# Contiguous value casts, means on the matmul engine, keys in natural order and GpSimd kept to the norm's Newton steps, in a Sinkhorn-attention and Fourier-mix kernel

## The chip, the cores and the metric

The kernel runs on one core of a Trainium2 chip. The metric is device time in microseconds (us), the median over separate executions. The engines are named as in the profile: PE (TensorE matmul), PEld (its weight loads), DVE (VectorE), ACT (ScalarE), POOL (GpSimd), SP (SyncE). A profile is one execution; its span is some 2 us shorter than the measured time. A run that is over 1.5 per cent above the fastest of its kernel is called slow.

## The reference, cut to what matters

```python
P = sort_net                                   # (4, 8, 8, 8): batch, head, block, block
for _ in range(5):                             # Sinkhorn: rows, then columns
    P = exp(P - max(P)); P /= P.sum(-1); P /= P.sum(-2)
k_sorted = einsum('bhij,bhjcd->bhicd', P, k_b) # keys and values of 8 blocks of 96 are mixed
v_sorted = einsum('bhij,bhjcd->bhicd', P, v_b)
attn = softmax(q_b @ k_sorted.T / 8)           # each block of 96 queries sees its own block
x = (attn @ v_sorted)                          # -> (4, 768, 512)
X = real(fft(fft(x, axis=1), axis=2))          # Fourier mix over rows and columns
u = x + X;  un = (u - mean(u)) / sqrt(var(u) + 1e-6)
out = u + relu(un @ w_ch1) @ w_ch2             # 512 -> 2048 -> 512
```

## The kernel before

Batches 0 and 1 share the first half of V, batches 2 and 3 the second. The kernel subtracts the mean over the 96 rows of each source block from V, so that `exp(s) - 1` can be multiplied with it in fp16; the aim is to keep digits. The mean goes through the Fourier transform by a separate path of a few rows (`a_path`, `a_rows`). A scheduler orders the instructions of each engine from the program's dependences; each engine then runs its list in that order.

```python
    # V: mean by strided reduce, then centring, halves split between DVE and GpSimd
    def v_center(t):
        for hf in range(2):
            nc.vector.tensor_reduce(                                   # L274
                vs2[:, hf, :], vh[hf].rearrange("p c d -> p d c"), axis=AX.X, op=ALU.add)
        # ... sum of the halves, times 1/96 ...
        vo = vc16[:, 0:D * BLK].rearrange("p (d r c) -> p c r d", r=6, c=16)
        for hf in range(2):
            eng = nc.vector if hf == 0 else nc.gpsimd
            eng.tensor_tensor(vo[:, 8 * hf:8 * hf + 8], ...,           # L286
                              op=ALU.subtract)   # fp16 written with a 192-byte step along d

    # attention, for each head pair
            # keys mixed on PE, evicted from PSUM row by row (c innermost, contiguous)
            dst = ks[:, :, 3 * half:3 * half + 3, :].rearrange("p i r c -> p r i c")
            if half == 0: nc.scalar.copy(dst, src)                     # L389
            else:         nc.vector.tensor_copy(dst, src)              # L391
            # q transposed on PE out of a copy that GpSimd made
            for h2 in range(2):            # one head after the other
                # 2 x (4 score matmuls, Exp on ACT, minus 1 on DVE (L423))
                # 12 AV matmuls, 65 columns wide; normalise

    # Fourier mix: fold on DVE (plus part) and GpSimd (minus part), then PE

    # layer norm: reciprocal square root by three Newton steps, all on DVE
            for _ in range(3):
                nc.vector.tensor_tensor(z, y, y, op=ALU.mult)
                nc.vector.scalar_tensor_tensor(z, z, -0.5, x, op0=ALU.mult, op1=ALU.mult)
                nc.vector.scalar_tensor_tensor(y, z, 1.5, y, op0=ALU.add, op1=ALU.mult)
    # then un (DVE), four PE transposes per 128 rows, ut (DVE), and the MLP on PE
```

The softmax here doesn't subtract the row's maximum and nothing guards it: scores larger than these inputs give would overflow.

## Time and profile before

| | before |
|---|---|
| time, median of 3 runs | 455.73 us (455.05 to 459.06) |
| span of the profile, mean granted clock | 452.6 us, 0.896 |
| first MLP matmul | 172.9 us |
| last matmul ends | 448.1 us |

The kernel has two phases. Up to the first MLP matmul, batch 0 has to go through sorting, attention, Fourier mix and norm with little for PE to do. From then on the MLP of one batch is interleaved with the attention of the next, and PE is nearly always busy. The table of stretches shows that (columns: stretch, its length, busy time and instructions of each engine, granted PE clock, DMA share, GB/s):

```profile
0.00:60.00 60.00, 2.87 (x14) 2.87 (x14) 47.86 (x39) 2.56 (x6) 26.93 (x22) 1.00 0.96 241
60.00:120.00 60.00, 15.99 (x147) 13.72 (x146) 56.00 (x39) 8.36 (x21) 35.49 (x11) 0.74 0.06 9
120.00:173.00 53.00, 32.28 (x279) 21.48 (x279) 36.16 (x82) 8.95 (x20) 17.37 (x14) 0.59 0.18 23
...
172.90:448.10 275.20, 258.74 (x1987) 144.24 (x1985) 161.63 (x395) 99.64 (x217) 56.27 (x49) 0.97 0.15 35
```

In the first phase DVE is the busy engine, not PE. The timeline shows with what (columns: start, duration, engine, line, operation, out<-in, shapes, and in brackets the idle time before it and who ended it). These are the DVE and POOL lines of the centring and of the exp-minus-1 that came after it:

```profile
19.19 30.08 DVE L286 TENSOR_TENSOR vc_127<-v_83,vb_215 128x3072 f16<-128x3072 f32 x1
19.14 15.45 POOL L286 TENSOR_TENSOR vc_127<-v_85,vb_215 128x3072 f16<-128x3072 f32 x1 [8.94 <-DVE vb_215 L280]
...
89.48 15.40 DVE L286 TENSOR_TENSOR vc_127<-v_962,vb_1579 128x3072 f16<-128x3072 f32 x1
89.47 30.14 POOL L286 TENSOR_TENSOR vc_127<-v_964,vb_1579 128x3072 f16<-128x3072 f32 x1 [0.19 <-POOL rb_105 L347]
104.45 15.39 DVE L423 TENSOR_SCALAR ebuf_119<-ex_403 96x384 f16<-96x384 f32 x1
```

In the first pair POOL ends at 34.6 and DVE at 49.3, 14.7 us later; in the second DVE ends at 104.9 and POOL at 119.6, again 14.7 us later. Whichever was second took twice as long: the two did not run side by side, one waited for the other. The exp-minus-1 on DVE, 0.49 us elsewhere, ends at 119.84, just after POOL does. By what means one engine holds up the other, the traces do not show.

### The profile page before, as it was taken

Reading aid. Unit: us, or ns where it says so; the run is one execution under the profiler, and the core shown is the slowest. Engines: PE = TensorE matmul, PEld = TensorE weight load, DVE = VectorE, ACT = ScalarE, POOL = GpSimd, SP = SyncE. Lnnn points to the kernel's source line nnn. Section 1 sums busy time; section 2 is a strip of 40 time slices with the busy share of each in tenths; the row PEclk is TensorE's granted clock in tenths of the full one; section 3 lists DMA queues with packets and bytes.
Section 4 is the critical chain, followed back from the end, with each engine's and each line's share of the span. In section 5 each row is a group of like instructions: output and inputs, shape, how many; then the busy total and the mean of one; then the engine's idle time right before and its main releaser. Section 6 shows DMA issues by size and latency. Waiting matters only on the chain.

```text
span 452.6 us, 6022 instructions
## 1 busy us (share of the span) xinstructions
PE 309.8 (68%) x2420; PEld 182.3 (40%) x2420; DVE 302.2 (67%) x553; ACT 119.5 (26%) x264; POOL 136.1 (30%) x96
## 2 busy tenths in 40 slices
PE   0000065400366459996999999979999979999996
PEld 0000065300244325653554655545456544545452
DVE  3999858999857677689654857858277777451101
ACT  1000005200122103631340753323146403406150
POOL 8390010499521910325500042290001082000000
PEclk9999999955555579999899999969999979999999
DMA  9999520200035000442001023500010000010101
GB/s 285 302 216 190 199 98 2 35 0 0 0 38 70 0 0 2 58 75 56 25 0 48 24 36 46 109 25 0 25 47 1 25 25 23 2 51 21 70 1 70
DMA packets 16549, 26.00 MB, mean 57 GB/s; under 512 B 1220, under 2 KB 11656, under 8 KB 16008
## 3 DMA queue, kind: packets, MB, share of 16 engines
q0 software_dynamic: 11040, 10.49, 15.4%
q1 hardware_dynamic: 5336, 13.55, 8.1%
q10 hardware_dynamic: 144, 1.57, 1.0%
q8 instruction: 19, 0.31, 0.3%
q14 instruction: 10, 0.08, 0.1%
HBM read 29.80 MB, written 6.29 MB: 80 GB/s over the span
## 4 chain that ended last, share of the span: by engine, by line
PE 42%; DVE 40%; DMA 7%; POOL 4%; issue 4%; ACT 2%; SPq 0%; DVEq 0%; ACTq 0%
DVE vc_127 L286 10%; DVE ebuf_119 L423 5%; DMA v_962<-in_v_dram 3%; POOL pmt_135 L456 3%; DMA v_85<-in_v_dram 2%; DVE ebuf_121 L423 2%; DVE vsb_131 L307 1%; DVE vs_1_1576 L274 1%; DVE vs_0_212 L274 1%; PE pm_2760 L563 1%; PE pm_4167 L563 1%; PE pm_3821 L563 1%; PE pm_2895 L563 1%; PE pm_1969 L563 1%; PE pm_4013 L563 1%
## 5 line engine op out<-in xcount | busy, mean ns | idle before, releaser
L556 PEld LDWEIGHTS <-w1sb 128*128 128x128 f16 x512 | 48.8, 98 | 31.6 <-issue 1.0
L242 PE MATMUL pf_180<-id_sb,pdup_178 32*128 32x32 f32 x16 | 3.6, 397 | 57.1 <-DVE pdup_178 L233 57.1
L286 POOL TENSOR_TENSOR vc_127<-v_964,vb_1579 128x3072 f16<-128x3072 f32 x1 | 30.1, 30142 | 0.2 <-POOL rb_105 L347 0.2
L286 DVE TENSOR_TENSOR vc_127<-v_83,vb_215 128x3072 f16<-128x3072 f32 x1 | 30.1, 30080 | 0.0
L242 PEld LDWEIGHTS pf_180<-id_sb,pdup_178 32*128 32x128 f32 x16 | 3.5, 325 | 57.1 <-DVE pdup_178 L233 57.1
L431 PEld LDWEIGHTS <-ebuf_119 96*128 96x128 f16 x192 | 8.5, 105 | 43.1 <-DVE ebuf_119 L423 42.5
L431 PE MATMUL pf_414<-vsb_129,ebuf_119 96*128 96x65 f16 x12 | 0.9, 244 | 31.3 <-DVE ebuf_119 L423 31.3
L286 POOL TENSOR_TENSOR vc_127<-v_85,vb_215 128x3072 f16<-128x3072 f32 x1 | 15.5, 15452 | 8.9 <-DVE vb_215 L280 8.9
L286 DVE TENSOR_TENSOR vc_127<-v_962,vb_1579 128x3072 f16<-128x3072 f32 x1 | 15.4, 15405 | 0.0
L423 DVE TENSOR_SCALAR ebuf_119<-ex_403 96x384 f16<-96x384 f32 x1 | 15.4, 15390 | 0.0
L218 ACT ACTIVATE pw<-pw 32x64 f32<-32x64 f32 x5 | 1.3, 255 | 51.2 <-DVE pw L225 50.1
L298 PEld LDWEIGHTS <-vc_127 128*128 128x128 f16 x128 | 9.9, 110 | 9.0 <-issue 8.1
L431 PEld LDWEIGHTS <-ebuf_121 96*128 96x128 f16 x192 | 8.7, 105 | 10.8 <-DVE ebuf_121 L423 10.3
L350 POOL COPY bdd_2965<-bdv_1_208 128x256 f32<-128x256 f32 x1 | 0.4, 397 | 41.6 <-PE pf_2038 L354 41.6
L393 POOL COPY qr_3090<-q_2954 128x768 f16<-128x768 f16 x1 | 0.8, 822 | 31.1 <-PE pf_2998 L398 31.1
L411 PEld LDWEIGHTS <-ksb_123 64*128 64x128 f16 x128 | 6.8, 100 | 7.6 <-issue 5.9
L567 DVE TENSOR_TENSOR u_3503<-pm_4129,u_3503 128x512 f32<-128x512 f32 x1 | 0.7, 691 | 13.2 <-PE pm_4129 L563 13.2
L416 ACT ACTIVATE ex_437<-pf_432 96x384 f32<-96x384 f32 x1 | 0.5, 486 | 32.0 <-PE pf_432 L411 32.0
L411 PEld LDWEIGHTS <-ksb_125 64*128 64x128 f16 x128 | 7.0, 103 | 4.7 <-issue 3.2
L274 DVE TENSOR_REDUCE vs_1_1576<-v_962 128x64 f32<-128x3072 f32 x1 | 5.3, 5289 | 5.3 <-DMA v_962<-in_v_dram 5.3
L567 DVE TENSOR_TENSOR u_3429<-pm_3975,u_3429 128x512 f32<-128x512 f32 x1 | 0.7, 692 | 11.2 <-PE pm_3975 L563 11.2
L237 POOL COPY pdup_190<-pw 32x1024 f32<-32x1024 f32 x1 | 1.5, 1547 | 21.8 <-DVE pw L225 21.8
(1455 smaller groups left out, 949.0 us busy)
## 6 DMA issues: line engine op xcount, KB each, us to landing
w1sb<-in_moe_w_ch_dram POOLq DMA_DIRECT2D x1, 2048.0 KB, 35.7
w2sb<-in_moe_w_ch_dram POOLq DMA_DIRECT2D x1, 2048.0 KB, 57.5
v_83<-in_v_dram ACTq DMA_DIRECT2D x1, 1536.0 KB, 6.8
v_85<-in_v_dram SPq DMA_DIRECT2D x1, 1536.0 KB
v_962<-in_v_dram SPq DMA_DIRECT2D x1, 1536.0 KB, 13.1
v_964<-in_v_dram SPq DMA_DIRECT2D x1, 1536.0 KB, 16.3
cd_sb<-k_cd SPq DMA_DIRECT2D x1, 514.0 KB
sd_sb<-k_sd SPq DMA_DIRECT2D x1, 514.0 KB
```

The costliest lines, as they stand in the source:

```text
L237: nc.gpsimd.tensor_copy(pdup.rearrange("p i (g j) -> p i g j", j=NB), pw[:, :, None, :].broadcast_to([32, NB, 16, NB]))
L242: nc.tensor.matmul(ps[:, i, :], pdup[:, i, :], id32)
L274: nc.vector.tensor_reduce(vs2[:, hf, :], vh[hf].rearrange("p c d -> p d c"), axis=AX.X, op=ALU.add)
L286: eng.tensor_tensor(vo[:, 8 * hf:8 * hf + 8], vh[hf].rearrange("p (c r) d -> p c r d", r=6), vb[:, 0:1, :][:, None, :, :].broadcast_to([12 ...
L298: nc.tensor.matmul(ps[:, dd, :], vc16[:, BLK * d:BLK * d + 128], bdv16[t].rearrange("p g i -> p (g i)"))
L307: nc.vector.tensor_copy(dst, src)
L411: nc.tensor.matmul(ps[:, j, :], ks[rows, 4 * g + j].rearrange("p r c -> p (r c)"), qt[rows, :, cc])
L423: nc.vector.tensor_scalar(ed, ex.rearrange("p j r c -> p j c r"), -1.0, None, op0=ALU.add)
L431: nc.tensor.matmul(po[:, 65 * T:65 * T + 65], e[:, S * g + 256 * tt + 128 * n: S * g + 256 * tt + 128 * n + 128], vs[:, 8 * h + 4 * g + tt ...
L456: nc.gpsimd.tensor_tensor(m_[:, :, 0:DM], rt[:, 0:3, :], rt[:, 3:6, :], op=ALU.subtract)
L556: nc.tensor.matmul(ps, w1sb[:, c, 128 * fc:128 * fc + 128], ut[:, c, :], start=(c == 0), stop=(c == 3))
L563: nc.tensor.matmul(ps, hr[:, fc, 128 * tt:128 * tt + 128], w2sb[:, fc, :], start=(fc == 0), stop=(fc == 15))
```

## The change

The intent is to take the long strided work off DVE and POOL in the first phase and to shorten the attention chain.

- V is cast to fp16 contiguously: for the first half on ACT without subtracting the mean, whose share PE then subtracts in `v_mix` (64 more matmuls); for the second half on DVE, with a tree of adds for the mean. The mean of the first half is 12 fp32 products with an identity on PE.
- Keys stay in natural order, so the mixed keys are evicted with a 12-byte step.
- GpSimd loses the folds, the reversed copies and the q copies. It gets the Newton steps of the norm.
- The scores of two heads are computed together, half of the exp-minus-1 moves to ACT, and AV streams are 96 columns wide instead of 65 (the result layout lets them overlap).

The diff, cut to its core:

```diff
-    def v_center(t):                                # strided reduces and centring, gone
+    def v_mean(t):
+        if t == 0:
+            for n in range(12):
+                nc.tensor.matmul(ps..., idf, v32[t, n // 6][...], start=(n == 0), stop=(n == 11))
+        else:
+            # 3 adds of 1024 and 4 adds of 1536 to 192 elements on DVE
+    def v_cast(t):
+        for n in range(8):
+            if t == 0: nc.scalar.copy(dst, src)
+            else:      nc.vector.tensor_tensor(dst, src, vbs[t]..., op=ALU.subtract)
     def v_mix(t):
-                nc.tensor.matmul(ps[:, dd, :], vc16[:, BLK * d:BLK * d + 128], bdv16[t]...)
+                nc.tensor.matmul(ps[:, dd, :], vcx[:, :, d], bd, ...)     # weights: 128-byte step
+                if t == 0:
+                    nc.tensor.matmul(ps[:, dd, :], vbn[:, d:d + 1].broadcast_to([128, 128]), bd, ...)
...
-                dst = ks[:, :, 3 * half:3 * half + 3, :].rearrange("p i r c -> p r i c")
+            dst = ks[:, :, 0:BLK].rearrange("p i (c r) -> p r i c", r=6)[:, 3 * half:3 * half + 3]
...
-            nc.gpsimd.tensor_copy(
+        nc.vector.tensor_copy(
             qr, q16[:, 2 * hl:2 * hl + 2].rearrange("p h r d -> p r h d"))
...
+                if h2 == 0: nc.vector.tensor_scalar(ed, src, -1.0, None, op0=ALU.add)
+                else:       nc.scalar.activation(ed, src, AF.Identity, bias=negone[0:96])
...
-                            po[:, 65 * T:65 * T + 65],
+                        po[:, 65 * T:65 * T + 96],
...
+            nc.gpsimd.tensor_scalar(xh, x, -0.5, None, op0=ALU.mult)
             for _ in range(3):
-                nc.vector.tensor_tensor(z, y, y, op=ALU.mult)
-                nc.vector.scalar_tensor_tensor(z, z, -0.5, x, ...)
-                nc.vector.scalar_tensor_tensor(y, z, 1.5, y, ...)
+                nc.gpsimd.tensor_tensor(z, y, y, op=ALU.mult)
+                nc.gpsimd.tensor_tensor(z, z, xh, op=ALU.mult)
+                nc.gpsimd.tensor_scalar(z, z, 1.5, None, op0=ALU.add)
+                nc.gpsimd.tensor_tensor(y, z, y, op=ALU.mult)
```

## The prediction

> **What bounds the kernel now.** Two phases. Until 172.9 us (first MLP matmul, timeline) PE is mostly idle: the stretch table gives it 2.9 us busy in 0-60, 0.1 in 105-120. From 172.9 on PE is busy 68.7 of 74.3, 76.9 of 82.8, 73.1 of 78.0 and 40.1 of 44.6 us: PE-bound.
>
> The chain of waits in phase one: the centring write with a 2-byte stride (L286) holds DVE 30.0 us (19.2-49.3) while only one of five Sinkhorn rounds is done; the scheduler then pulls the second half's reduce and centring (5.3 + 5.4 + 15.4 us) ahead of attention; GpSimd's 30.1 us share makes one DVE exp-minus-1 take 15.4 us instead of 0.49 (105-120); attention of batch 0 takes 7.75 us per head pair; FFT, norm 25 us.
>
> [...] besides that 15.4 us, DVE's mirrored add takes 2.9-3.3 us for 771 elements beside GpSimd work, though the 1536-element add took 0.97.
>
> **The change, costed (estimates from these durations).**
> - Removed: L286 (30 + 15.4 on DVE, 45.6 on POOL), strided reduces (21.3), the POOL collision.
> - Added at the start: 12 fp32 means on PE. The 257-wide fp32 product takes two records of 0.21 us, so 512 wide about 0.85 warm: 10-13 us. ACT casts, 8 x about 0.8 us, hidden. v_mix(0) gets 64 more matmuls: 8-11 us instead of 6.3.
> - The order of instructions shows a new risk: a DVE copy of q stands in front of the Sinkhorn sums. Before, q landed at 20 us; now perhaps 17-18, so Sinkhorn ends near 27 rather than the 12 it could.
> - Then transposes to 32 us, means to 44, first scores to 48, v_mix to 57, attention of batch 0 (about 6.3 us per pair, since two heads' exps share one chain) to 78, FFT and norm (DVE alone, with 7 us of second-half centring interleaved) to 108.
> - Phase two: PE work nearly equal. 12 AV matmuls take 0.70 us, 0.058 each, near the 0.055 of 128-column v_mix matmuls, so they look bound by the stationary side[...]. So 96-wide streams are free. Saved: about 1 us per batch of row products (L354), perhaps 1 us of scores, and 2-3 us per FFT, where PE now waits for GpSimd's pmt, ee and oo (3.9 + 1.8 + 1.9 us). ACT gains about 8 us per batch, POOL's norm chain is a little slower; both hidden by MLP.
>
> **Sum.** First MLP matmul from 172.9 to about 108: -65. Phase two 280 to about 268: -12. 452.6 - 77 = 376 span, about 378 us in time. Nearly all removed phase-one time is on the critical path; half comes back as Sinkhorn delay, means and v_mix.
>
> Predicted 378 us, 80% range 358 to 400. Faster by over 2%: 0.97; within: 0.02; slower: 0.01.
>
> **What would show it.** DVE idle 8-14 us near 4-18 us, released by q's DMA; PE busy with means 32-44; no DVE instruction over 3 us; first MLP matmul at 100-115; attention of batch 0 6-6.7 us per pair; AV spacing still about 0.06 us; PE idle before the FFT matmuls under 2 us in batches 1-3; the last stretch unchanged.
>
> **What would make it wrong.** Faster if q lands early or attention reaches 5 us per pair; slower if weight loads with a 128-byte column step cost more than contiguous ones, the second v load or the row DMAs arrive late (norm of batch 0 waits), ACT becomes the attention's limit, or the PE clock stays at half rate longer (it read 0.50 from 105 to 147).

The sum came to 378 us in time (452.6 - 65 - 12 = 376 of span, and 2 outside it). "96-wide streams are free" rests on the spacings of 0.058 and 0.055 us alone and is the author's estimate (experiment 5 tests it). Its "warm", like "cold" in an expectation below, stands for the granted clock: 1.00 or 0.50 in the traces.

## More of the kernel before

The norm's Newton steps on DVE take 0.16 us each and follow each other at 0.20 us:

```profile
163.76 0.17 DVE L522 TENSOR_SCALAR nx_848<-mv_814 128x3 f32<-128x3 f32 x1
...
164.37 0.16 DVE L529 TENSOR_TENSOR nz_850<-ny_849 128x3 f32<-128x3 f32 x1
164.57 0.16 DVE L530 SCALAR_TENSOR_TENSOR nz_850<-nz_850,nx_848 128x3 f32<-128x3 f32 x1
164.76 0.16 DVE L532 SCALAR_TENSOR_TENSOR ny_849<-nz_850,ny_849 128x3 f32<-128x3 f32 x1
...
166.14 0.55 DVE L537 TENSOR_SCALAR un_864<-u_821,mv_814,ny_849 128x512 f16<-128x512 f32 x1
```

and the evictions of the mixed keys take half a microsecond on either engine:

```profile
181.66 0.48 ACT L389 CAST ksb_123<-pf_985 128x384 f16<-128x384 f32 x1
...
181.52 0.56 DVE L391 CAST ksb_123<-pf_993 128x384 f16<-128x384 f32 x1 [1.05 <-PE pf_993 L380]
```

## The result, and the profile after

| | before, same rounds | after |
|---|---|---|
| time, median of 4 runs | 455.39 us (453.6 to 459.06) | 410.08 us (409.12 to 411.62) |
| span, granted clock | 452.6 us, 0.896 | 408.5 us, 0.923 |
| first MLP matmul | 172.9 us | 121.1 us |
| first MLP matmul to last matmul | 275.2 us | 283.5 us |

The ratio is 0.8999 (95 per cent interval 0.8936 to 0.9061). A ratio is the mean time of one kernel's fast runs over the mean time of the other's fast runs of the same rounds, so it is not quite the ratio of the medians. The change is a clear gain, but 410 us lies outside the predicted range of 358 to 400. The last two rows say where the miss of 32 us sits: the first phase was predicted to end at 108 us and ended at 121.1 (+13); the second was predicted to shrink by 12 and grew by 8 (+20).

The same stretches as before:

```profile
0.00:60.00 60.00, 27.65 (x210) 19.80 (x210) 23.95 (x57) 20.98 (x33) 23.47 (x31) 1.00 0.94 224
60.00:121.00 61.00, 35.61 (x296) 23.58 (x297) 43.99 (x88) 17.51 (x28) 6.45 (x16) 0.64 0.30 66
...
121.10:404.60 283.50, 252.87 (x1947) 141.71 (x1945) 143.60 (x304) 127.22 (x237) 25.82 (x99) 0.97 0.15 34
```

In the second phase PE has 5.9 us less to do than before (252.87 against 258.74) and yet needs 8.3 us more. The idle time of PE between its matmul records, put down to the kind of matmul that came after each gap, tells which wait grew:

| PE idle after the first MLP matmul, us, in front of | before | after |
|---|---|---|
| the Fourier mix | 10.3 | 0.0 |
| the transposes of the normalised rows | 3.1 | 16.3 |
| AV | 1.7 | 9.7 |
| the MLP's first product | 0.7 | 3.8 |
| all | 16.5 | 30.6 |

The Fourier mix behaves as predicted. The norm does not: the transposes of its output now wait 16.3 us. The POOL timeline shows the chain, and the PE timeline what it did to PE:

```profile
170.69 0.17 DVE L585 TENSOR_SCALAR nx_1504<-mv_1470 128x3 f32<-128x3 f32 x1
170.95 0.24 POOL L586 TENSOR_SCALAR nh_1507<-nx_1504 128x3 f32<-128x3 f32 x1 [20.30 <-DVE nx_1504 L585]
171.35 0.19 POOL L593 TENSOR_TENSOR nz_1506<-ny_1505 128x3 f32<-128x3 f32 x1 [0.15 <-DVE ny_1505 L589]
171.62 0.20 POOL L594 TENSOR_TENSOR nz_1506<-nz_1506,nh_1507 128x3 f32<-128x3 f32 x1
171.90 0.23 POOL L595 TENSOR_SCALAR nz_1506<-nz_1506 128x3 f32<-128x3 f32 x1
172.22 0.20 POOL L596 TENSOR_TENSOR ny_1505<-nz_1506,ny_1505 128x3 f32<-128x3 f32 x1
...
174.72 0.55 DVE L600 TENSOR_SCALAR un_1525<-u_1477,mv_1470,ny_1505 128x512 f16<-128x512 f32 x1 [3.46 <-POOL ny_1505 L596]
```

```profile
175.32 0.40 PE L605 MATMUL pf_1527<-idh_sb,un_1525 128*128 128x128 f16 x4 [2.38 <-DVE un_1525 L600]
175.56 0.33 PE L619 MATMUL pm_1936<-ut_1009,w1sb 128*128 128x384 f16 x1
```

From the variance term to the normalised rows, the norm took 2.4 us before (163.76 to 166.14) and takes 4.0 us here (170.69 to 174.72); where a cast on DVE runs beside it, as in the group at 125 us, it is 4.8 us. There are thirteen GpSimd instructions in place of nine on DVE, and they follow each other at 0.27 to 0.32 us instead of 0.20. PE waits 2.38 us at 175.32 although more of the MLP (L619, at 175.56) stands right behind: what it multiplies had been complete since 132.9 us. PE takes its matmuls in order, and the scheduler had put the transposes there. Over the seven groups the wait grew by 1.9 us each, close to the 1.6 us by which the chain grew.

The first phase again, from the start. The DVE copy of q, predicted as a risk, is there, and it has a second side (DVE, POOL and DVE lines):

```profile
17.57 3.28 DVE L440 COPY qr_266<-q_86 128x768 f16<-128x768 f16 x1 [14.17 <-DMA q_86<-in_q_dram]
...
13.72 6.92 POOL L208 MEMSET vsf<- 1x8192 f16 x1
...
64.12 0.34 DVE L440 COPY qr_609<-q_124 128x768 f16<-128x768 f16 x1
```

The same copy takes 0.34 us when POOL is idle. At 17.57 it runs until 20.85, 0.2 us after GpSimd's memset of one partition ends (20.64): the same blocking as before, started now by a memset. The sorting then ends at 29.3 us (27 predicted). After it comes what was predicted of PE, almost to the microsecond (PE timeline):

```profile
30.02 0.39 PE L265 MATMUL pf_193<-idh_sb,pdup_189 32*128 32x32 f16 x8 [30.02 <-DVE pdup_189 L256]
...
33.93 7.47 PE L298 MATMUL pf_225<-v_78,idf_sb 128*128 128x512 f32 x12
41.23 5.31 PE L298 MATMUL pf_225<-v_81,idf_sb 128*128 128x512 f32 x12
46.48 0.36 PE L427 MATMUL pf_250<-bdk_202,k_84 128*64 128x128 f16 x6
```

| end of, us | predicted | after |
|---|---|---|
| sorting | 27 | 29.3 |
| means on PE | 44 | 46.5 |
| first scores begin | 48 | 49.1 |
| value mixing of the first half | 57 | 59.3 |
| attention of batch 0 | 78 | 83.9 |
| Fourier mix and norm (first MLP matmul) | 108 | 121.1 |

Against the prediction, the delay grows by 3.6 us between the value mixing and the end of attention, and by 7.2 us in the Fourier mix and norm. In attention, the evictions of the mixed keys stand out. They answer to L389 and L391 of before:

```profile
132.99 1.46 ACT L436 CAST ksb_118<-pf_1043 128x384 f16<-128x384 f32 x1 [4.69 <-PE pf_1043 L427]
...
133.31 1.45 DVE L438 CAST ksb_118<-pf_1051 128x384 f16<-128x384 f32 x1 [0.36 <-PE pf_1051 L427]
```

They take three times as long as before, on both engines, for the same elements. In the Fourier mix and norm, the chain of waits runs through work of the second half of V (L308 and L313 are its mean, L600 is the end of batch 0's norm; columns: start, share of the chain in us, engine, tile and line):

```profile
101.75 1.11 DVE vcx L308
102.86 0.60 DVE st_907 L577
103.47 1.12 DVE vcx L308
104.59 0.09 DVE mv_876 L578
104.68 1.70 DVE vcx L313
...
112.22 0.55 DVE un_931 L600
```

### The profile page after: what moved, and what is told of

It reads as the page before. It is cut to its first block, busy times and chain, and to the rows that moved or that the text cites. A ratio compares the mean times of both kernels' runs of the same rounds, so it can differ in the third digit from the quotient of the medians.

```text
span 408.5 us, 6064 instructions
## 1 busy us (share of the span) xinstructions
PE 316.2 (77%) x2452; PEld 185.1 (45%) x2452; DVE 212.2 (52%) x449; ACT 165.7 (41%) x298; POOL 55.7 (14%) x146
## 3 DMA queue, kind: packets, MB, share of 16 engines
HBM read 30.92 MB, written 6.29 MB: 91 GB/s over the span
## 4 chain that ended last, share of the span: by engine, by line
PE 52%; DVE 18%; ACT 13%; DMA 6%; POOL 5%; issue 5%; POOLq 0%; DVEq 0%
DMA q_86<-in_q_dram 4%; PE pf_225 L298 3%; ACT ebuf_114 L476 3%; ACT ebuf_106 L476 2%; DVE ksb_118 L438 1%; PE pf_790 L387 1%; ACT ksb_118 L436 1%; PE pf_206 L278 1%; PE pm_3686 L626 1%; PE pm_4186 L626 1%; PE pm_3840 L626 1%; PE pm_2026 L626 1%; PE pm_2933 L626 1%; PE pm_4167 L626 1%; PE pm_4148 L626 1%
## 5 line engine op out<-in xcount | busy, mean ns | idle before, releaser
L619 PEld LDWEIGHTS <-w1sb 128*128 128x128 f16 x512 | 48.7, 99 | 34.5 <-issue 5.4
L347 PEld LDWEIGHTS <-vcx 128*128 128x128 f16 x128 | 15.6, 187 | 0.1
L622 ACT ACTIVATE hr_1775<-pm_1776 128x384 f16<-128x384 f32 x1 | 0.5, 491 | 32.2 <-DVE ny_990 L587 32.2
L440 DVE COPY qr_266<-q_86 128x768 f16<-128x768 f16 x1 | 3.3, 3283 | 14.2 <-DMA q_86<-in_q_dram 14.2
L491 PEld LDWEIGHTS <-ebuf_110 97*128 97x128 f16 x96 | 5.3, 106 | 8.9 <-DVE ebuf_110 L474 8.9
L491 PEld LDWEIGHTS <-ebuf_102 97*128 97x128 f16 x96 | 5.1, 102 | 8.5 <-DVE ebuf_102 L474 7.2
L350 PEld LDWEIGHTS <-vbn 128*128 128x128 f16 x64 | 8.7, 135 | 0.0
L622 ACT ACTIVATE hr_3743<-pm_3744 128x384 f16<-128x384 f32 x1 | 0.5, 491 | 18.8 <-PE pm_3744 L619 18.8
L233 ACT ACTIVATE pw<-pw 32x64 f32<-32x64 f32 x5 | 1.3, 255 | 15.9 <-DVE pw L240 15.3
L491 PEld LDWEIGHTS <-ebuf_114 97*128 97x128 f16 x96 | 5.5, 108 | 4.8 <-ACT ebuf_114 L476 4.6
L630 DVE TENSOR_TENSOR u_3517<-pm_4148,u_3517 128x512 f32<-128x512 f32 x1 | 0.7, 691 | 13.2 <-PE pm_4148 L626 13.2
L298 PE MATMUL pf_225<-v_78,idf_sb 128*128 128x512 f32 x12 | 7.5, 787 | 0.0
L626 PEld LDWEIGHTS <-hr_1929 128*128 128x128 f16 x48 | 4.7, 98 | 5.6
L626 PEld LDWEIGHTS <-hr_2836 128*128 128x128 f16 x48 | 4.7, 98 | 5.5
L626 PEld LDWEIGHTS <-hr_4051 128*128 128x128 f16 x48 | 4.7, 98 | 5.5
L626 PEld LDWEIGHTS <-hr_3897 128*128 128x128 f16 x48 | 4.7, 98 | 5.5
L626 PEld LDWEIGHTS <-hr_3743 128*128 128x128 f16 x48 | 4.7, 98 | 5.6
L626 PEld LDWEIGHTS <-hr_3589 128*128 128x128 f16 x48 | 4.7, 102 | 5.2 <-issue 0.3
L208 POOL MEMSET vsf<- 1x8192 f16 x1 | 6.9, 6922 | 0.1
## 6 DMA issues: line engine op xcount, KB each, us to landing
w1sb<-in_moe_w_ch_dram POOLq DMA_DIRECT2D x1, 2048.0 KB, 16.5
tab_775<-k_sd SPq DMA_DIRECT2D x1, 514.0 KB, 15.8
```

What stands on the lines that cost most here:

```text
L208: nc.gpsimd.memset(vsb[96:97, :, 0:D], 0.0)
L298: nc.tensor.matmul(ps.rearrange("p c d -> p (c d)"), idf, v32[t, n // 6][:, 8 * (n % 6):8 * (n % 6) + 8, :].rearrange("p c d -> p (c d)"), ...
L347: nc.tensor.matmul(ps[:, dd, :], vcx[:, :, d], bd, start=True, stop=(t == 1))
L350: nc.tensor.matmul(ps[:, dd, :], vbn[:, d:d + 1].broadcast_to([128, 128]), bd, start=False, stop=True)
L491: nc.tensor.matmul(po[:, 65 * T:65 * T + 96], e[:, S * g + 256 * tt + 128 * n: S * g + 256 * tt + 128 * n + 128], vsf[:, vi:vi + 96], star ...
L619: nc.tensor.matmul(ps, w1sb[:, c, 128 * fc:128 * fc + 128], ut[:, c, :], start=(c == 0), stop=(c == 3))
```

## The experiments

All kernels below start from the changed kernel ("after") and gave the reference's result, except where said. Each was timed in 4 to 6 runs beside runs of the kernel before. "Idle" is PE's idle time after the first MLP matmul, as in the table above.

### 1. The norm's Newton steps back on DVE (e1_norm_dve)

My theory was that the GpSimd norm is the second phase's loss. The rival was that ACT's new work, or the wider AV, delays PE, and the norm only shows it.

```diff
-            nc.gpsimd.tensor_scalar(xh, x, -0.5, None, op0=ALU.mult)
-                nc.gpsimd.tensor_tensor(z, y, y, op=ALU.mult)
-                ... three more on gpsimd
+                nc.vector.tensor_tensor(z, y, y, op=ALU.mult)
+                nc.vector.scalar_tensor_tensor(z, z, -0.5, x, op0=ALU.mult, op1=ALU.mult)
+                nc.vector.scalar_tensor_tensor(y, z, 1.5, y, op0=ALU.add, op1=ALU.mult)
```

> One undo: the twelve small operations of the reciprocal root return from GpSimd to DVE as nine. Theory A (the norm's latency on GpSimd is what PE waits for before its transposes; PE idle before them is 16.3 us after the first MLP matmul, 3.1 in the kernel before): that idle falls to about 4 us, time about 398, most of it in batches 1 to 3; in batch 0 nothing, because the chain then shares DVE with the second half's centring. Theory B (the attention is held by ACT, and the norm's wait only moves): the idle moves to the AV matmuls, time within 3 us of 410.

Measured: 389.44 us (388.89 to 390.44), ratio to before 0.8534 (0.851 to 0.8559). That is 20.6 us less than after. The idle time before the norm's transposes fell from 16.3 to 2.0 us, and all idle time from 30.6 to 13.2. The PE and stretch views:

```profile
124.87 4.71 PE L618 MATMUL pm<-ut,w1sb 128*128 128x384 f16 x28
129.72 0.40 PE L604 MATMUL pf<-idh_sb,un 128*128 128x128 f16 x4
...
124.90:383.90 259.00, 245.82 (x1947) 138.21 (x1945) 150.57 (x363) 127.41 (x237) 6.25 (x8) 1.00 0.16 37
```

What follows: the second phase goes from 283.5 to 259.0 us, a gain of 24.5. About 17 us are idle time, and 7 us are PE's own busy time, 252.9 to 245.8 for the same 1947 matmuls. The granted clock in that stretch rose from 0.97 to 1.00. The stretch views of after tie the fall of the clock to the waits, here for the wait that ended at 259.01 us (stretch, length, busy time of the engines, then the granted clock):

```profile
256.55:259.96 3.41, 0.95 (x11) 0.71 (x12) 1.52 (x4) 0.49 (x1) 1.32 (x7) 1.00 0.16 61
259.96:263.37 3.41, 3.41 (x14) 1.58 (x13) 1.12 (x3) 0.49 (x1) 0.00 (x0) 0.50 0.00 0
```

In after, three of the seven waits (ended at 259.01, 286.42 and 331.55) are followed within a microsecond by such a half-rate stretch of 3.41 us; in experiment 1 none is. In all sixteen traces the clock changes on a grid of 3.41 us. In the second phases, a full-rate stretch of that grid in which PE was idle for 59 per cent or more, by its matmul records, was followed by half rate 32 times out of 32; one with 58 per cent or less never was (1175 stretches, 19 of them 30 per cent idle or more). Before and after alone have 7 of the 32, at 62 per cent or more, and 143 of the others, at 50 per cent or less. So a wait of 2.1 to 2.5 us costs some 1.7 us more, or nothing, depending on how it falls on the grid (an estimate: half of 3.41 us). Three such stretches, and the 6.83 us at half rate from 126.84 less the 2.5 us of waiting in them, come to about 7 us, which is PE's extra busy time.

The theory stands: experiments 3 and 5 take back the two rival changes and leave the waits before the transposes at 15.8 and 15.9 us. One thing is not separated. Each build is scheduled anew, and PE's list changed with the edit: the transposes of the second of the seven groups stand after 68 products of the MLP's first stage in after, and after 86 here. No run kept the norm on GpSimd and put its transposes later. One thing went the other way, against the expectation of no change in batch 0: the first MLP matmul came later, at 124.9 instead of 121.1. Experiment 7 returns to that.

### 2. Keys and values in the old row order (e2_keys_rc)

```diff
-            dst = ks[:, :, 0:BLK].rearrange("p i (c r) -> p r i c", r=6)[:, 3 * half:3 * half + 3]
+            dst = ks[:, :, 0:BLK].rearrange("p i (r c) -> p r i c", c=16)[:, 3 * half:3 * half + 3]
```

(The value casts write the same order, in runs of 64 elements, and stay as cheap: 0.82 us on ACT and 0.95 on DVE, as in after.)

> One undo: keys again in the order (r, c), so the eviction of the mixed keys writes runs of 32 bytes; the cast of V writes rows of 64 elements in the same order, so the result stays right. Theory A (a write with a 12-byte step is what makes this eviction 1.44 us instead of 0.5): the eviction goes to about 0.5 us on ACT and DVE, attention of batch 0 gets about 0.9 us shorter per pair, PE idle before AV matmuls falls by a few us, time about 404. Theory B (the two evictions slow each other because they run together on one PSUM bank or on two engines): they stay over 1 us.

Measured: 402.58 us, the median of three fast runs (402.29 to 403.11; the fourth, 408.98, is slow), ratio 0.8822 (0.8795 to 0.8848). That is 7.5 us less than after. The profiled execution is the slow one (span 407.2 us), so mainly the durations of ACT and DVE instructions are read from it:

```profile
130.71 0.48 ACT L439 CAST ksb<-pf 128x384 f16<-128x384 f32 x1 [4.60 <-PE pf L430]
...
131.03 0.56 DVE L441 CAST ksb<-pf 128x384 f16<-128x384 f32 x1 [0.36 <-PE pf L430]
```

What follows: the 12-byte write step alone triples the eviction, to 1.45 us on either engine against 0.48 on ACT and 0.56 on DVE. Theory B falls: the two evictions still overlap here (131.03 to 131.19 us), and both are short. What it cost in time is less clear, because the granted clock differs as well: 0.934 to 0.936 in the fast runs, 0.922 to 0.925 in after. In the profiled execution, with 0.920 and five half-rate stretches after a wait where after has three, the first MLP matmul still came 2.3 us sooner than in after (118.8), and PE's idle time was 1.7 us less (28.9). So about 4 us (an estimate from these two) belong to the write; the rest of the 7.5 us goes with the clock, and whether the edit raised the clock or the grid fell well was not tested. My prediction never costed this write.

### 3. The exp-minus-1 back on DVE (e3_exp_dve)

```diff
-                if h2 == 0: nc.vector.tensor_scalar(ed, src, -1.0, None, op0=ALU.add)
-                else:       nc.scalar.activation(ed, src, AF.Identity, bias=negone[0:96])
+                nc.vector.tensor_scalar(ed, src, -1.0, None, op0=ALU.add)
```

> One undo: exp minus 1 of the second head goes back from ACT (0.96 us each) to DVE (0.49). If ACT is the attention's limit (theory B of the first run), PE idle before AV (9.7 us after the first MLP matmul) falls to about 3 us and attention of batch 0 gets about 1 us shorter per pair: time about 401. If ACT's load is hidden by the MLP (the prediction's theory), time stays within 3 us of 410.

Measured: 411.04 us (406.35 to 411.78), ratio 0.9011 (0.8984 to 0.9038): no difference from after (0.8999). The wait moved: idle before AV fell from 9.7 to 4.6 us, idle before the scores rose from 0.9 to 5.5. On ACT the operation takes 0.95 us, on DVE 0.49. So which engine does it makes no difference to the time here. (The profiled execution was faster than the four others, 406.35 against 410.83 to 411.78 us, at a higher clock, 0.937 against 0.923; its span is not used. Its trace has one half-rate stretch after a wait for the norm where after has three: one kernel varies by 4 to 5 us with the clock.)

### 4. The first q copy on GpSimd, out of DVE's list (e4_q_pool)

```diff
-        nc.vector.tensor_copy(
+        eng = nc.gpsimd if (b, hp) == (0, 0) else nc.vector
+        eng.tensor_copy(
             qr, q16[:, 2 * hl:2 * hl + 2].rearrange("p h r d -> p r h d"))
```

> One undo: only the first copy of q goes back to GpSimd, behind its DMA issues; nothing else is moved. Theory A (Sinkhorn waits for q's DMA because the copy stands in front of it on DVE): DVE's idle of 14.2 us before that copy is gone, Sinkhorn ends at 13 to 18 us instead of 29.3, all later stages come 10 to 13 us earlier, time about 398. Rival: V's and the weights' DMAs or PE's cold clock then hold the means, and the time falls by less than 4 us.

Measured: 400.94 us (400.37 to 402.26), ratio 0.8788 (0.8762 to 0.8814), 9.1 us less than after. The transposed sorting matrix reaches PE at 21.3 us instead of 30.0, and the first MLP matmul comes at 111.7 instead of 121.1, while the second phase keeps its length (283.6 us). So one copy of 0.34 us of work, put in front of the sorting, cost 9 us: 14.17 us of waiting for q's transfer and 3 us of waiting for the memset, less what the sorting needed anyway. DVE's next large cast is now the one that meets the memset: the copy of the sorting matrix (L256) takes 3.84 us there at 17.38, against 0.68 in after, where the memset was over.

### 5. AV streams 65 wide again (e5_av65)

```diff
-                        po[:, 65 * T:65 * T + 96],
+                        po[:, 65 * T:65 * T + 65],
-                        vsf[:, vi:vi + 96], start=(n == 0), stop=(n == 1),
+                        vsf[:, vi:vi + 65], start=(n == 0), stop=(n == 1),
```

> One undo: AV streams 65 columns wide again, nothing else. The prediction's theory (the stationary load sets the pace, so the 31 more columns are free): spacing of AV matmuls stays at 0.058 us, PE's time in them stays near 14 us after the first MLP matmul, time within 2 us of 410. Rival (the streams cost PE time): time falls by 3 to 5 us. Second rival (the wider streams keep the granted clock up): the clock falls below 0.92 and the time rises.

Measured: 409.22 us (408.4 to 410.54), ratio 0.8986 (0.8955 to 0.9018): the same as after. PE's own time in AV after the first MLP matmul fell from 14.0 to 11.4 us, so the stationary side does not fully hide 96 columns; the prediction's reason was not quite right. The equal time is a balance of two phases. The first MLP matmul came 4.3 us sooner (116.8), and the second phase took 4.1 us longer (287.6), at a granted clock of 0.953 there against 0.970 in after, with 2.7 us more of waiting in front of the scores (0.9 to 3.6) and six half-rate stretches after a wait for three. So the second rival, the clock, is not excluded, and what the wider streams cost at an equal clock was not shown.

### 6. The mean's rows inside attention: a miss (e6_apath)

The first half's mean path (`a_path`, fp32 products of 6.1 us) stands between attention and the Fourier mix of batch 0 in after, from 84.37 to 90.48. Nothing in it needs attention, so it was called after the second head pair.

```diff
             av(b, hp, es)
+            if b == 0 and hp == 1:
+                a_path(0); a_rows(0); a_rows(1)
```

> One move: the fp32 products of the mean rows of batch 0 (4.4 + 1.9 us on PE between the last AV and the first FFT matmul) and their row DMAs are issued inside attention of batch 0, after the second pair. If they are what delays the FFT of batch 0, its first matmul follows the last division by about 3 us instead of 6.5, the wait for the row DMA (2.4 us) goes, and the first MLP matmul comes about 5 us earlier: time about 405. If the norm chain or the second V load holds that stage, less than 2 us.

Measured: 411.31 us (410.66 to 411.95), ratio 0.9029 (0.8992 to 0.9066). The expected gain did not come. Moving the call changed the whole order: the products came at 68.0 us, between AV and the next pair's keys, and the Fourier mix began at 98.8 instead of 90.4 us. The first MLP matmul came at 126.1 us, and the second phase was 3.8 us shorter. Two things were changed at once by the scheduler, so this run says nothing clean about the products; it says that a call cannot be moved alone.

### The three parts together (e7_three)

Experiments 1, 2 and 4 in one kernel.

> Three undos together: norm on DVE, keys in (r, c) order, first q copy on GpSimd. Measured alone they gave 20.6, 7.2 and 9.1 us. If they act at different places of the chain they add up: about 373 us. If the norm's stalls and the others cover each other: 380 or more.

Measured: 375.77 us (375.0 to 376.44), ratio 0.8254 (0.8214 to 0.8293). The three single gains are 20.6 + 7.5 + 9.1 = 37.2 us (the expectation had 7.2, from a median with the slow run in it); together they give 34.3. This is the predicted time, but part of that is luck: the prediction had accepted the q copy in front of the sorting, and its removal makes up for what the first phase still lost elsewhere. The first MLP matmul comes at 111.9 (108 predicted), and the second phase takes 257.2 us.

### 7. What holds batch 0's norm

What is left of the first phase's miss shows on PE in the kernel with the three parts undone:

```profile
103.65 0.61 PE L608 MATMUL pf<-idh_sb,un 128*128 128x128 f16 x4 [14.67 <-DVE un L603]
```

Its chain of waits has the second half's casts (L335, eight of them) between the Newton steps of the first norm:

```profile
97.50 0.07 DVE nz L595
97.57 0.87 DVE vcx L335
98.44 0.07 DVE nz L596
98.51 0.87 DVE vcx L335
99.38 0.07 DVE ny L598
```

DVE takes its list in order, so each small step waits for a cast that the norm does not need. This fits what experiment 1 did to the first phase: its DVE list has six casts in front of the first normalised rows (115.36 us), where after, with the steps on GpSimd, has one (112.22). Two kernels tested it. The first (e8_few) takes the mean of the second half from three rows only (wrong result, relative error 0.65), which removes seven adds:

```diff
-            # 3 adds of 1024 elements, 4 adds of 1536 to 192
-            src = tr[:, 0:3]
+            src = v32[t, 1][:, 45:48]
```

> e7_three, but the second half's mean is taken from three of its 96 key rows only, so seven vector adds (1.1 + 1.1 + 1.1 + 1.7 + 0.9 + 0.5 + 0.3 = 6.7 us) are gone. WRONG RESULT on purpose for batches 2 and 3 (the mean that is subtracted is no longer the mean). Theory C: in e7_three the second half's mean and casts stand on DVE in front of batch 0's first norm and are what PE's 14.7 us wait before the first norm transposes is made of. Then first transposes 103.7 to about 98, time 375.8 to about 370. Rival D: that wait is the norm and the row path's own chain, and the adds only fill its holes. Then 374 to 377.

Measured: 370.94 us (368.54 to 371.24), ratio 0.8129 (0.8098 to 0.8161), 4.8 us less. The norm's first transposes came at 101.0 instead of 103.7 us, the first MLP matmul at 108.0 instead of 111.9. The second kernel (e9_hold) keeps the result and holds the casts back with a one-element copy out of the first normalised group:

```diff
+        if t == 1:
+            nc.vector.tensor_copy(vb[:, 0, 0:1], uns[0, 0][:, 0, 256:257])
         nc.vector.tensor_reduce(vb[:, 0, :], src.rearrange("p c d -> p d c"), axis=AX.X, op=ALU.add)
```

> e7_three, with one 1-element copy of the first normalised, transposed group into the second half's mean, so that its eight casts (0.87 us each) cannot come before the first norm. Theory C: first transposes from 103.7 to about 97.5; first MLP from 111.9 to about 106; the first MLP evictions, whose buffer is the second half's V, then wait for the casts, which gives back 2 us or so. Time 370 to 373. Rival D: 375 to 378, or worse by the later casts.

Measured: 378.14 us (377.62 to 378.67), ratio 0.8299 (0.8274 to 0.8325): 2.4 us slower. Its PE lines show both halves of the story:

```profile
100.20 1.06 PE L610 MATMUL pf<-idh_sb,un 128*128 128x128 f16 x8 [9.94 <-DVE un L605]
...
107.12 2.11 PE L624 MATMUL pm<-ut,w1sb 128*128 128x384 f16 x12
115.52 1.44 PE L624 MATMUL pm<-ut,w1sb 128*128 128x384 f16 x4 [6.29 <-ACT hr L627]
```

The norm did come earlier: the transposes waited 9.94 us instead of 14.67, and the first MLP matmul came 4.8 us sooner, at 107.1. Then the MLP stopped for 6.29 us, because its first output buffer is the memory of the second half's V, which the held casts still had to read. I had expected that to give back 2 us. So the theory about the wait holds, and the cure does not pay as long as the two share a buffer. In after itself the same sharing shows as 3.8 us of idle time before the MLP's first product: its first eviction on ACT begins at 126.02 us, and the last cast ends at 125.94.

### Towards a better version

Five more kernels kept the vector norm and the row order of keys. `q` is transposed head by head out of its own tile ("no copy") or copied on GpSimd for the first pair, and the twelve mean products may be called before the sorting, where PE is idle.

```diff
+    psm0 = pf([128, 8, D])                       # in front of the sorting
+    for n in range(12):
+        nc.tensor.matmul(psm0..., idf, v32[0, n // 6][...], start=(n == 0), stop=(n == 11))
...
-        nc.vector.tensor_copy(qr, q16[...])      # "no copy"
         for r in range(6):
-            nc.tensor.matmul(ps[:, r, :], qr[:, r]..., idh, is_transpose=True)
+            for h2 in range(2):
+                nc.tensor.matmul(ps[64 * h2:64 * h2 + 64, r, :], q16[:, 2 * hl + h2, r, :], idh,
+                                 is_transpose=True)
```

With the means first, no copy, and also the mean's rows inside attention as in experiment 6 (b2_best):

> A version meant to beat both: norm on DVE, keys in (r, c) order, q transposed per head without a copy, PE's fp32 means issued before the Sinkhorn rounds' products, mean-row products inside attention of batch 0. Means from about 14 to 27 us, first key mixing at 31 instead of 46.5, first MLP matmul at about 98, time about 361. If V lands late or DVE waits for the means in front of other work, the first key mixing comes at 37 and the time is about 367.

It took 373.24 us (373.2 to 373.98), ratio 0.8197 (0.8164 to 0.823), less gain than either expectation. The means were done by 23.1 us instead of 46.5 in after, but the Fourier mix still began only at 81.5; between the second and the third pair PE waited 5.48 us for the transfer of the mean path's table. Without the rows inside attention (b1_mean_first):

> This is b2_best without the early row path: vector norm, keys row by row, q transposed per head without a copy, means on PE in front of the sorting. Theory A: the early row path is what lost the 12 us that the early means won (b2 put its fp32 products between head pairs and let the second half's mean into the attention). Then this run is near e7_three (375.8) minus most of 12, say 364 to 368, first MLP matmul near 100 to 103 against e7's 111.9. Theory B: the means are not the limit of the first phase after that; whatever order, attention of batch 0 is held by the same ACT and DVE work. Then 372 to 376, first MLP near 106 to 111.

It took 367.93 us (367.4 to 368.34), ratio 0.8084 (0.8059 to 0.811). The Fourier mix began at 65.9 us and the first MLP matmul came at 101.1, as theory A said. This is the fastest correct kernel: 42 us less than after.

No copy of q, but the means where they were (b4_q_heads):

> e7_three with q transposed head by head straight from q's tile (no copy on any engine) in place of the GpSimd copy of the first pair. If only the copy in front of the sorting counts, this equals e7_three within 1 per cent (372 to 379). If DVE's later q copies (16 of them less the first) matter too, 2 to 4 us less. PE does 12 transposes of a pair in place of 6, so PE busy may rise about 3 us over the kernel.

It took 378.95 us (378.27 to 379.56), ratio 0.8325 (0.8301 to 0.8348), 3.2 us slower than the GpSimd copy. Twelve transposes in place of six took PE 7.0 us instead of 5.4 in the second phase. With the GpSimd copy and the means first (b9_means_first):

> e7_three with the means placed on PE in front of the sorting (as b1, but with the q copies kept and the first on GpSimd). b4_q_heads was 3.2 us slower than e7_three, so if head-by-head transposes cost that here too, 367.9 - 3.2 = about 365; if not, 368.

It took 371.02 us (370.91 to 371.26), ratio 0.8144 (0.8124 to 0.8163). Here the copy is the slower choice by 3.1 us, opposite to the pair before. The traces show two costs. In the second phase the transposes per head lose both times: 260.6 us against 257.2 (b4 against e7), and 260.6 against 256.9 (b1 against b9). In the first phase of b9, DVE's list holds a later copy of q in front of the exp-minus-1 of the last head pair. DVE stood idle for 7.70 us until that q had landed (64.29), AV waited 7.64 us in turn, and the Fourier mix began at 75.0 us instead of 65.9. It is the same kind of wait as in experiment 4. No run took it away alone. The last one adds the hold of experiment 7 (b10_hold):

> b9_means_first with the hold of e9_hold. If both hold as theory C says: about 361. Rival D: 365 to 368.

It took 373.39 us (371.94 to 374.26), ratio 0.8192 (0.8163 to 0.822), again about 2.4 us slower than without the hold, with the same two effects (first MLP matmul 5.5 us earlier, 6.2 us of idle time in the MLP's first product).

## Why the prediction was wrong, point by point

The direction was right and so was most of the first phase. The total was off by 32 us, in these steps.

- **"POOL's norm chain is a little slower; both hidden by MLP."** This is the step that failed most. The chain grew from 2.4 to 4.0 us or more, and it was not hidden: PE's list put the transposes at a fixed place, and the seven groups of the second phase waited 16.3 us in all, 13.2 more than before. Undoing it alone gave 20.6 us (experiment 1: 24.5 gained in the second phase, 3.8 lost in the first), the size of the second phase's whole miss. About 17 us of the 24.5 were PE's idle time and 7 the lower clock. With it undone the second phase takes 259.0 us, which is 16 less than before; the predicted saving was 12. "Hidden" was taken from PE being busy on average. What decides is whether the waiting instruction stands in PE's list before or after work that is ready.
- **A write that was not costed.** "Keys in natural order" appears in the change and nowhere in the sum. The eviction went from 0.48 and 0.56 to 1.45 us, and undoing it gave 7.5 us, of which the traces put about 4 on the write (experiment 2). The trace of before already held a warning in kind, the strided centring (15.4 us for 3072 elements a row, where the contiguous casts of after take 0.95 for 768), which was costed only as something removed. (The prediction calls its step 2 bytes; in the code it is 192.)
- **"Sinkhorn ends near 27."** It ended at 29.3. The wait for q was predicted as 8 to 14 us and measured 14.17, a right call. Not foreseen were the 3.28 us of a 0.34-us copy beside a GpSimd memset, although the prediction named that very blocking for the kernel before. Whoever sees that two engines block each other has to look for the next pair that will overlap.
- **"FFT and norm (DVE alone, with 7 us of second-half centring interleaved) to 108."** The right thing was named, with the wrong size. After attention it took 37.2 us instead of 30. The second half's mean and casts put about 15 us on DVE, half in the seven adds (1.23, 1.19, 1.21, 1.76, 0.96, 0.56 and 0.36 us) and half in the eight casts (0.95 each). In after, the chain holds 5.4 us of the adds (L308 and L313 in the lines above). Once the Newton steps are back on DVE, the casts stand in front of the first norm too (experiment 7: the kernel is 4.8 us faster without the adds; the first MLP matmul comes 4.8 us earlier when the casts are held). Another 6.1 us are fp32 products in front of the Fourier mix; their own cost could not be isolated (experiment 6).
- **"About 6.3 us per pair."** The pair ends in after are at 61.9, 69.9, 76.1 and 83.0 us, 7.0 us on average; with the three parts undone they are at 52.8, 59.3, 65.5 and 72.5, 6.6 us (each at the end of the pair's last reciprocal). The difference goes with the key evictions: undone alone they give 6.5 us (experiment 2), the q copy alone leaves 7.0 (experiment 4).
- **Right:** the means on PE (12.6 us; 10 to 13 predicted), the value mixing (9.8 us; 8 to 11 predicted), PE idle before the Fourier matmuls (10.3 to 0.0 us), the last stretch (PE busy 40.1 of the last 44.6 us before, 40.7 after), and ACT's growth (99.6 to 127.2 us in the second phase), as taking back half of the exp-minus-1 changed nothing (experiment 3).
- **"Perhaps 1 us of scores."** Pairing the heads took PE's time in scores from 10.9 to 5.4 us in the second phase, more than predicted, but PE's idle time before AV grew from 1.7 to 9.7, so nothing was gained there. That wait stayed in every kernel here except where it moved to the scores (experiments 3 and 5); what would shorten it was not found.
- **Right in the total, with a reason that was too strong:** going back from 96-wide AV changes the time by less than 1 us, but it is not free on PE. It takes 2.6 us there, and the total hides two phases that moved in opposite ways (experiment 5).
- **Named as a risk and present:** weight loads with a 128-byte column step take 187 ns, against 110 for the same product before and 98 in the MLP. The value mixing stayed within its range all the same.

## What to carry to other kernels

Small dependent steps belong on the engine that runs them fastest (here 0.20 us a step on DVE against 0.27 to 0.32 on POOL), even when that engine is busy and another is idle: they are latency, and moving them costs a wait wherever the next engine's list has its fixed place for the result (here 1.9 us more in each of seven places). The exception here is batch 0, where the busy engine's list had casts between the steps (experiment 7). Before calling such a chain hidden, look at which instruction of the in-order list will wait and what stands behind it. When a layout change turns a contiguous write into a scattered one, cost that write first (here 0.48 and 0.56 us became 1.45), and look at early instructions in a list (a copy in front of the sorting, casts of the second half in front of the first norm) for waits that nothing in the source text shows.
